# q in rows of 6 KB, row-tiled transposes and a new token order in an attention kernel with a token mixer

## Chip, cores, metric

One core of one Trainium2 chip. The metric is the device time of one execution in microseconds. Times are medians of several executions; every ratio to the kernel before uses executions on the same chip in the same rounds.

## The reference

```python
# q (8, 16, 384, 64), k and v (8, 4, 384, 64), scaled by 0.1; w_out (1024, 1024)
k = np.repeat(k, 4, axis=1); v = np.repeat(v, 4, axis=1)
scores = np.matmul(q, k.transpose(0, 1, 3, 2)) / np.sqrt(64)
attn = softmax(scores)                                    # over the last axis
x = np.matmul(attn, v).transpose(0, 2, 1, 3).reshape(8, 384, 1024)
wq, wk = x @ w_q, x @ w_k                                 # (8, 384, 64)
W_tok = wq @ wk.T / np.sqrt(64)                           # per batch, (384, 384)
out = np.maximum(W_tok @ x, 0.0) @ w_out                  # float32
```

The kernel never forms W_tok. It computes wk^T x first (`mix_c`), then multiplies by wq (`mix_m`), then by w_out (`po`).

One warning for all that follows. The scores are so small that the softmax is nearly flat, and the rows of a batch of the result differ from their mean by only 0.9% (norm, worked out from the reference). Rows stored in wrong places give an error of 1.3%, which the comparison of the runs let pass. So "correct" in these runs says that values are right, and says nothing of the order of the tokens. Where an experiment puts rows in wrong places on purpose this is said; where it claims the right order, that follows from the indices, not from a run.

## The kernel before

A Python function writes one fixed order of instructions per engine. It keeps a small model of the clocks of the engines (`clk`, `ready`) and at each step issues the TensorE work that the model calls ready. If nothing is, it issues filler matmuls (`keep_busy`) that hold the array's clock up. The parts that matter, with cuts marked:

```python
def load(b):                                   # q: three tokens per partition and head, 768 B
    def ld(dst, src, a, z, c0=0, c1=C):
        nc.sync.dma_start(out=dst[:, a:z, c0:c1],
                          in_=src[b, a:z].rearrange("h (p c) d -> p h c d", p=P)[:, :, c0:c1])
    # ... b == 0: k, q in slices of c, v, by halves of the heads; else k, q, q, v

def tr_q(b, blocks):                           # full 128x128 transposes, one PSUM bank, one copy
    # ...
    nc.tensor.transpose(out=ps[:, n * G + j, :], in_=qb[:, c, kp, j]..., identity=ident)
    nc.vector.tensor_copy(out=QT[:, t0:t0 + 2 * G, :], in_=ps)

def scores(b, s):                              # two heads side by side in row tiles, then exp
    nc.tensor.matmul(out=ps[:, u, :], lhsT=KT[lo:hi, kp * C + kc, :],
                     rhs=QT[lo:hi, t0:t0 + G, :].rearrange("k i p -> k (i p)"), ...)
    nc.scalar.activation(out=pt..., in_=ps, func=AF.Exp, scale=attn_scale)

def po():                                      # output projection, copy to SBUF, store
    dst = out[b].rearrange("(p c) n -> c p n", c=C)[c]
    # ...
    nc.sync.dma_start(out=dst, in_=osb)        # 128 rows of 4 KB
```

A chain per batch (`chain_open`) goes x transposes, `wqk`, `wk_tr`, `mix_c`, four `mix_m`, then 48 `po` matmuls. K and Q of batches 2 to 7 and most of x are transposed by DMA; the first two batches and the last third of each x by TensorE.

The softmax here doesn't subtract the row's maximum and nothing guards it: scores larger than these inputs give would overflow.

Of the kernel before, what the change touches and what calls it, by code (L numbers as in the profile page):

```python
# [15 lines left out]
def kernel(  # L16
# [17 lines left out]

    nc = tc.nc
# [9 lines left out]
    NH = 512  # L45
    KP = Hkv // 2
# [3 lines left out]
    NWIDE = 0  # L50
    NB = 4
    NPT = 9
    EAGER = 1
    DMA_TR = 5500
# [24 lines left out]
    clk = {"pe": 0.0, "dve": 0.0, "act": 0.0}  # L79
    mode = ["full"]  # L80
    wide_ps = [psG.tile([P, 2, NH], F32, name=f"wide{i}") for i in range(NWIDE)]
    bank_ps = [psG.tile([P, NH], F32, name=f"bank{i}") for i in range(NB)]
    wide_free = [0.0] * NWIDE
# [16 lines left out]

    def when(*keys):
        return max(ready.get(key, INF) for key in keys)
# [4 lines left out]

    def wide():
        return min((f, i) for i, f in enumerate(wide_free))
# [12 lines left out]
    def load(b):  # L122
        kraw = raw_p.tile([P, Hkv, C, D], F32, name="kraw")
        vraw = raw_p.tile([P, Hkv, C, D], F32, name="vraw")
        qraw = raw_p.tile([P, Hq, C, D], F32, name="qraw")
        raws[b] = (kraw, vraw, qraw)

        def ld(dst, src, a, z, c0=0, c1=C):
            nc.sync.dma_start(out=dst[:, a:z, c0:c1],  # L129
                              in_=src[b, a:z].rearrange("h (p c) d -> p h c d", p=P)[:, :, c0:c1])  # L130

        half = Hq // KP
        if b == 0:
            ld(kraw, k, 0, 2)
            ld(qraw, q, 0, half, 0, 1)
            ld(qraw, q, 0, half, 1, C)
            ld(vraw, v, 0, 2)
            ld(kraw, k, 2, 4)
            ld(qraw, q, half, Hq)
            ld(vraw, v, 2, 4)  # L140
        else:
            ld(kraw, k, 0, 4)
            ld(qraw, q, 0, half)
            ld(qraw, q, half, Hq)
            ld(vraw, v, 0, 4)

    def cast_open(b):
        nats[b] = (nat_p.tile([P, KP, C, 2, D], BF16, name="kb"),
                   nat_p.tile([P, C, KP, G, 2, D], BF16, name="qb"))

    def cast_k(b, kp, eng):
        for u in range(2):
            eng.tensor_copy(out=nats[b][0][:, kp, :, u, :], in_=raws[b][0][:, 2 * kp + u])  # L153

    def cast_q(b, kp, eng):
        for u in range(2):
            h0 = (2 * kp + u) * G
            eng.tensor_copy(out=nats[b][1][:, :, kp, :, u, :].rearrange("p c i d -> p i c d"),  # L158
                            in_=raws[b][2][:, h0:h0 + G])

    def cast_qc(b, kp, c, u, copy):
        h0 = (2 * kp + u) * G
        copy(out=nats[b][1][:, c, kp, :, u, :], in_=raws[b][2][:, h0:h0 + G, c, :])

    def cast_v(b, kp, eng):
        eng.tensor_copy(out=vexts[b % 3][:, 2 * kp:2 * kp + 2, :, :D],
                        in_=raws[b][1][:, 2 * kp:2 * kp + 2])

    def cast(b):
        cast_open(b)  # L170
        for kp in range(KP):
            cast_k(b, kp, nc.gpsimd)
        for kp in range(KP):
            cast_q(b, kp, nc.gpsimd)
        for kp in range(KP):
            cast_v(b, kp, nc.gpsimd)
# [4 lines left out]
    def start_tr(b):  # L181
        KT = tr_p.tile([P, KP * C, P], BF16, name="KT")
        QT = tr_p.tile([P, C * KP * G, P], BF16, name="QT")
        trs[b] = (KT, QT)

    def tr_dma(b, part):
        kb, qb = nats[b]
        KT, QT = trs[b]
        if part == 0:
            nc.sync.dma_start_transpose(out=KT, in_=kb.rearrange("p a c u d -> p (a c u d)"))  # L190
            for kp in range(KP):
                ready["K", b, kp] = clk["pe"] + DMA_TR
        else:
            c, n = part - 1, KP * G
            nc.sync.dma_start_transpose(out=QT[:, c * n:(c + 1) * n, :],
                                        in_=qb[:, c].rearrange("p a i u d -> p (a i u d)"))
            for kp in range(KP):
                ready["Q", b, kp, c] = clk["pe"] + DMA_TR

    def tr_k(b, kp0, kp1):  # L200
        kb, _ = nats[b]
        KT, _ = trs[b]
        _, i = bank()
        ps = bank_ps[i].bitcast(BF16).rearrange("p (n t) -> p n t", n=8)
        n = 0
        for kp in range(kp0, kp1):
            for c in range(C):
                nc.tensor.transpose(out=ps[:, n, :], in_=kb[:, kp, c].rearrange("p u d -> p (u d)"),
                                    identity=ident)
                n += 1  # L210
        nc.vector.tensor_copy(out=KT[:, kp0 * C:kp1 * C, :], in_=ps[:, :n, :])
        done = bank_free[i] = on("dve", 360 if n == C else 560, pe(56 * n))
# [3 lines left out]
    def tr_q(b, blocks):  # L216

        _, qb = nats[b]
        _, QT = trs[b]
        _, i = bank()  # L220
        ps = bank_ps[i].bitcast(BF16).rearrange("p (n t) -> p n t", n=8)
        for n, (c, kp) in enumerate(blocks):
            for j in range(G):
                nc.tensor.transpose(out=ps[:, n * G + j, :],
                                    in_=qb[:, c, kp, j].rearrange("p u d -> p (u d)"), identity=ident)
        end = pe(56 * G * len(blocks))
        if len(blocks) == 2 and blocks[1][0] == blocks[0][0]:
            t0 = (blocks[0][0] * KP + blocks[0][1]) * G
            nc.vector.tensor_copy(out=QT[:, t0:t0 + 2 * G, :], in_=ps)
            done = on("dve", 690, end)  # L230
        else:
            for n, (c, kp) in enumerate(blocks):
                t0 = (c * KP + kp) * G
                nc.vector.tensor_copy(out=QT[:, t0:t0 + G, :], in_=ps[:, n * G:(n + 1) * G, :])
                done = on("dve", 420, end)
        bank_free[i] = done
        for c, kp in blocks:
            ready["Q", b, kp, c] = done


    def groups(b):
        if b == 0:
            return [(kp, c) for kp in range(KP) for c in range(C)]
# [6 lines left out]
    def scores(b, s):  # L250
# [5 lines left out]
        for u in range(2):  # L256
            lo, hi = u * D, (u + 1) * D
            t0 = (c * KP + kp) * G
            nc.tensor.matmul(out=ps[:, u, :], lhsT=KT[lo:hi, kp * C + kc, :],  # L259
                             rhs=QT[lo:hi, t0:t0 + G, :].rearrange("k i p -> k (i p)"),  # L260
# [10 lines left out]
    def attend(b, g, u):  # L271
# [3 lines left out]
        if g == 0 and u == 0:  # L275
            xnats[b] = x_p.tile([P, C, Hq, D], BF16, name="xnat", bufs=3)
# [3 lines left out]
        for i in range(G):  # L280
            for kc in range(C):
                nc.tensor.matmul(out=ps[:, i * DE:i * DE + D + 1], lhsT=tiles[kc][:, u, i, :],  # L282
                                 rhs=vext[:, 2 * kp + u, kc, :D + 1],
# [4 lines left out]
        h0 = (2 * kp + u) * G  # L288
        nc.vector.tensor_tensor(out=xnats[b][:, c, h0:h0 + G, :], in0=avv[:, :, :D],  # L289
                                in1=rcp.to_broadcast([P, G, D]), op=ALU.mult)  # L290
# [9 lines left out]
    def x_by_dma(b, c):  # L300
        return b > 0 and c < C - 1
# [8 lines left out]
    def x_tr_dma(b, c):  # L310
        x_open(b)
        xn = xnats[b].rearrange("p c h d -> p c (h d)")
        nc.sync.dma_start_transpose(out=xTs[b][:, :, c, :], in_=xn[:, c, :])
        ready["T", b, c] = when(("X", b, c, 0), ("X", b, c, 1)) + DMA_TR

    def x_tr(b, c):
        x_open(b)
        xn = xnats[b].rearrange("p c h d -> p c (h d)")
        _, i = bank()
        ps = bank_ps[i].bitcast(BF16).rearrange("p (n t) -> p n t", n=DC)  # L320
        for dc in range(DC):
            nc.tensor.transpose(out=ps[:, dc, :], in_=xn[:, c, dc * P:(dc + 1) * P], identity=ident)  # L322
# [326 lines left out]
```

## Time and profile before

| | before |
|---|---|
| median (lowest to highest) | 222.12 us (221.69 to 222.29) |
| span of the profiled execution | 224.3 us |
| TensorE busy | 95% |
| VectorE, ScalarE busy | 65%, 63% |
| mean granted clock | 0.985 |
| last matmul starts | 220.5 us |

The profiled execution took 226.12 us and is of the slow state, by 1.8%. Three groups of the page: output projection, scores, and the copy of a finished half tile. After the bar stand busy time and the mean length of one in ns, then the idle time of the engine before them.

```profile
L408 PE MATMUL bank<-wout_sb,msb 128*128 128x512 bf16 x357 | 91.7, 382 | 1.3 <-issue 0.5
...
L259 PE MATMUL sc<-QT,KT 64*128 64x512 bf16 x288 | 47.5, 387 | 3.1 <-DMA QT<-qb 2.9
...
L421 DVE COPY osb<-bank 128x512 f32<-128x512 f32 (+1 forms) x49 | 33.1, 677 | 21.7 <-PE bank L408 20.5
```

A matmul's record of 380 ns includes its way through the pipeline; back to back they start every 216 ns. The copy takes 0.69 us, so a store of two halves becomes ready every 16 x 0.216 = 3.46 us when nothing but projection runs.

### The profile page before, as it was taken

What the parts mean: (1) busy time and instruction counts of PE and PEld (TensorE: products, weight loads), DVE (VectorE), ACT (ScalarE), POOL (GpSimd) and SP (SyncE); (2) the same over time, 40 slices, a digit from 0 to 9 for tenths busy, and PEclk for the clock granted to TensorE, in tenths of its full rate; (3) what the DMA queues carried; (4) which work ended last, traced back from release to release, by engine and by line L of the source; (5) the groups of instructions that cost most, each with busy time, mean ns of one, the idle gap of its engine ahead of it and who ended that gap; (6) DMA issues with size and microseconds to landing.
All of it is one profiled execution on the core that took longest, in us unless ns stands there. A gap on an engine that the chain in (4) does not pass through costs nothing.

```text
span 224.3 us, 5470 instructions
## 1 busy us (share of the span) xinstructions
PE 214.2 (95%) x2217; PEld 113.6 (51%) x2244; DVE 145.2 (65%) x365; ACT 140.6 (63%) x146; POOL 52.1 (23%) x97
## 2 busy tenths in 40 slices
PE   8999999589999999999999999999999999999993
PEld 5666665245545545454555546554555553434441
DVE  2355786834697758865887648874679569576332
ACT  3599998747788778887887887887888600000000
POOL 1385678406300540045016100620000000000000
PEclk9999999959999999999999999999999999999999
DMA  6996999999399979999999998989224422242424
GB/s 174 324 327 170 410 386 325 136 237 323 65 183 215 335 166 187 222 338 216 223 229 342 154 213 260 281 205 154 99 91 53 143 93 93 93 190 93 180 101 187
DMA packets 71688, 46.09 MB, mean 205 GB/s; under 512 B 42736, under 2 KB 67568, under 8 KB 71664
## 3 DMA queue, kind: packets, MB, share of 16 engines
q1 hardware_dynamic: 71520, 45.62, 77.6%
q8 instruction: 17, 0.28, 0.5%
q10 hardware_dynamic: 144, 0.13, 0.2%
q14 instruction: 7, 0.06, 0.1%
HBM read 23.59 MB, written 12.58 MB: 161 GB/s over the span
## 4 chain that ended last, share of the span: by engine, by line
PE 74%; DMA 14%; DVE 3%; SPq 3%; POOL 3%; issue 1%; DVEq 0%
PE bank L408 37%; PE bank L282 13%; PE sc L259 12%; DMA qraw<-in_q_dram 12%; PE bank L331 4%; SPq L129 3%; PE bank L384 3%; PE bank L362 2%; DMA QT<-qb 2%; PE bank L322 1%; POOL qb L158 1%; DVE osb L421 1%; PE bank L349 1%; DVE msb L389 1%; POOL wqk_sb L596 1%
## 5 line engine op out<-in xcount | busy, mean ns | idle before, releaser
L263 ACT ACTIVATE pt<-sc 128x1024 bf16<-128x1024 f32 x144 | 138.9, 1023 | 34.6 <-PE sc L259 34.4
L408 PE MATMUL bank<-wout_sb,msb 128*128 128x512 bf16 x357 | 91.7, 382 | 1.3 <-issue 0.5
L408 PEld LDWEIGHTS <-msb 128*128 128x128 bf16 x384 | 33.8, 98 | 42.4 <-issue 13.7
L259 PE MATMUL sc<-QT,KT 64*128 64x512 bf16 x288 | 47.5, 387 | 3.1 <-DMA QT<-qb 2.9
L282 PEld LDWEIGHTS <-pt 128*128 128x128 bf16 x1152 | 41.9, 98 | 15.8 <-issue 9.9
L282 PE MATMUL bank<-vext,pt 128*128 128x65 bf16 x1152 | 46.9, 195 | 0.4 <-DVE osb L421 0.2
L421 DVE COPY osb<-bank 128x512 f32<-128x512 f32 (+1 forms) x49 | 33.1, 677 | 21.7 <-PE bank L408 20.5
L289 DVE TENSOR_TENSOR xnat<-bank,rcp 128x256 bf16<-128x256 f32 x96 | 40.8, 425 | 3.3
L389 DVE TENSOR_SCALAR msb<-bank 128x384 bf16<-128x384 f32 x64 | 32.5, 551 | 9.5 <-PE bank L384 9.0
L287 DVE RECIPROCAL rcp<-bank 128x4 f32<-128x4 f32 x96 | 16.9, 176 | 17.6 <-PE bank L282 16.7
L158 POOL CAST qb<-qraw 128x768 bf16<-128x768 f32 x30 | 24.0, 827 | 17.4 <-DMA qraw<-in_q_dram 15.1
L153 POOL CAST kb<-kraw 128x192 bf16<-128x192 f32 x30 | 9.2, 347 | 67.3 <-DMA kraw<-in_k_dram 67.3
L259 PEld LDWEIGHTS <-KT 64*128 64x128 bf16 x288 | 12.4, 94 | 24.1 <-issue 17.2
L117 PE MATMUL bank<-idle 128*128 128x256 bf16 x80 | 14.8, 324 | 1.0 <-DVE idle L562 1.0
L331 PE MATMUL bank<-xT,wqk_sb 128*128 128x384 bf16 x64 | 11.7, 327 | 0.0
L117 PEld LDWEIGHTS <-idle 128*128 128x128 bf16 x80 | 7.9, 114 | 6.6 <-issue 4.0
L384 PE MATMUL bank<-wT,Csb 64*128 64x384 bf16 x32 | 10.6, 332 | 0.4 <-DVE rcp L287 0.3
L384 PE MATMUL bank<-wq,Csb 64*128 64x384 bf16 x32 | 10.6, 332 | 0.0
L599 POOL CAST wout_sb<-wld 128x1024 bf16<-128x1024 f32 x8 | 8.1, 1040 | 4.1 <-DMA wld<-in_moe_w_out_dram 4.1
L366 DVE CAST Csb<-bank 128x512 bf16<-128x512 f32 x8 | 5.5, 688 | 5.2 <-PE bank L362 5.2
L337 DVE CAST wT<-bank 128x384 bf16<-128x384 f32 x8 | 4.5, 558 | 6.7 <-PE bank L331 6.7
L323 DVE COPY xT<-bank 128x1024 bf16<-128x1024 bf16 x10 | 6.9, 688 | 2.5 <-PE bank L322 2.5
(33 smaller groups left out, 70.1 us busy)
## 6 DMA issues: line engine op xcount, KB each, us to landing
out_dram<-osb SPq DMA_DIRECT2D x23, 512.0 KB, 3.1
qraw<-in_q_dram SPq DMA_DIRECT2D x15, 768.0 KB, 7.4
wld<-in_moe_w_out_dram SPq DMA_DIRECT2D x4, 1024.0 KB, 9.5
kraw<-in_k_dram SPq DMA_DIRECT2D x7, 384.0 KB, 4.3
vraw<-in_v_dram SPq DMA_DIRECT2D x7, 384.0 KB, 8.9
qraw<-in_q_dram SPq DMA_DIRECT2D x1, 512.0 KB, 5.3
kraw<-in_k_dram SPq DMA_DIRECT2D x2, 192.0 KB, 3.7
vraw<-in_v_dram SPq DMA_DIRECT2D x2, 192.0 KB, 6.3
```

What stands on the lines that cost most here:

```text
L117: nc.tensor.matmul(out=bank_ps[i][:, :256], lhsT=idle[:, :P], rhs=idle, start=True, stop=True)
L158: eng.tensor_copy(out=nats[b][1][:, :, kp, :, u, :].rearrange("p c i d -> p i c d"), in_=raws[b][2][:, h0:h0 + G])
L259: nc.tensor.matmul(out=ps[:, u, :], lhsT=KT[lo:hi, kp * C + kc, :], rhs=QT[lo:hi, t0:t0 + G, :].rearrange("k i p -> k (i p)"), start=True, ...
L263: nc.scalar.activation(out=pt.rearrange("k u i p -> k u (i p)"), in_=ps, func=AF.Exp, scale=attn_scale)
L282: nc.tensor.matmul(out=ps[:, i * DE:i * DE + D + 1], lhsT=tiles[kc][:, u, i, :], rhs=vext[:, 2 * kp + u, kc, :D + 1], start=(kc == 0), sto ...
L287: nc.vector.reciprocal(out=rcp, in_=avv[:, :, D])
L289: nc.vector.tensor_tensor(out=xnats[b][:, c, h0:h0 + G, :], in0=avv[:, :, :D], in1=rcp.to_broadcast([P, G, D]), op=ALU.mult)
L331: nc.tensor.matmul(out=ps, lhsT=wqk_sb[:, dc, :], rhs=xT[:, dc].rearrange("d c p -> d (c p)"), start=(dc == 0), stop=(dc == DC - 1))
L384: nc.tensor.matmul(out=bank_ps[i][:, :S], lhsT=Csb[lo:hi, j * P:(j + 1) * P], rhs=w[lo:hi, :], start=True, stop=True)
L389: nc.vector.tensor_scalar_max(out=msb[:, dc, :], in0=bank_ps[i][:, :S], scalar1=0.0)
L408: nc.tensor.matmul(out=ps, lhsT=msbs[b][:, dc, c * P:(c + 1) * P], rhs=wout_sb[:, dc, half * NH:(half + 1) * NH], start=(nd == 0), stop=(n ...
L421: nc.vector.tensor_copy(out=osb[:, n0:n1], in_=ps[:, n0 - half * NH:n1 - half * NH])
```

## The change

The intent: q comes in packets of 6 KB instead of 768 B; TensorE's transposes are done as pairs of 64-row tiles, next to the scores, which use the same tiling; the x transposes of a batch start while its attention still runs; x has its columns in natural order. The price is a new order of tokens: a partition of q now holds one of 16 groups `s` of 24 tokens, so a tile of 128 queries has its column at `m * 16 + s`, and a tile's row goes to token `s * 24 + c * 8 + m` of the result. The core of the diff:

```diff
-        qraw = raw_p.tile([P, Hq, C, D], F32, name="qraw")
+        qraw = raw_p.tile([P, 2, C * M, D], F32, name="qraw")
+            src = q[b].rearrange("(u a) (s t) d -> (a s) u t d", u=2, t=C * M)
+            nc.sync.dma_start(out=qraw[:, :, c0 * M:c1 * M], in_=src[:, :, c0 * M:c1 * M])
 ... cut: casts by c, loads of batch 2 in the prologue, the model's DMA and GpSimd clocks
+    def half_trs(srcs):
+        two = [bank(half)[1] for half in range(2)]
+        for j, src in enumerate(srcs):
+            for half in range(2):
+                lo, hi = half * H, (half + 1) * H
+                nc.tensor.transpose(out=outs[half][:, j, :], in_=src[lo:hi], identity=ident[lo:hi, lo:hi])
+        return outs, two, pe(n * 29.5, "row")
+    def half_copies(outs, two, end, dsts, ns):
+                nc.vector.tensor_copy(out=dst[:, :, half * H:(half + 1) * H], in_=outs[half][:, n0:n1, :])
 ... cut: tr_k, tr_q, x_tr by these two; groups of batch 0 in the order of the others
-                             rhs=QT[lo:hi, t0:t0 + G, :].rearrange("k i p -> k (i p)"),
+                             rhs=QT[lo:hi, c * M:(c + 1) * M, kp * H:(kp + 1) * H].rearrange(
+                                 "k m (i s) -> k i m s", i=G),
 ... cut: xnat in natural column order; chain_open at the first attention of a batch
-        return b > 0 and c < C - 1
+        return b > XPE and c < C - 1          # XPE = 1: batch 1's x by TensorE too
 ... cut: wk_tr in a row tile
-        dst = out[b].rearrange("(p c) n -> c p n", c=C)[c]
+        dst = out[b].rearrange("(s c m) n -> c m s n", c=C, m=M)[c]
-                (...).dma_start(out=dst[:, n0:n1], in_=osb[:, n0:n1])
+                (...).dma_start(out=dst[:, :, n0:n1], in_=osb[:, n0:n1])
 ... cut: constants of the planner
```

## The prediction

> **What bounds the kernel now.** I read the busy line of the page first, then the 40 slices, then a table of windows, then the chain of waits around the one hole that the slices show, and last the groups, which give the duration of each operation that the change touches. The busy line and three rows of slices:
>
> ```profile
> PE 214.2 (95%) x2217; PEld 113.6 (51%) x2244; DVE 145.2 (65%) x365; ACT 140.6 (63%) x146; POOL 52.1 (23%) x97
> ...
> PE   8999999589999999999999999999999999999993
> ...
> ACT  3599998747788778887887887887888600000000
> ...
> PEclk9999999959999999999999999999999999999999
> ```
>
> TensorE looks full, but one slice (the eighth, 39 to 45 us) is half empty, the ninth runs at half clock, and ScalarE is at 9 only from about 11 to 34 us. So there are two regimes. In the first, the exponentials set the pace: the first starts at 7.55 us, there are 18 per batch at 1.023 us, so two batches last until about 7.5 + 36 x 1.023 = 44.3 us. In the second, from 50 us on, TensorE does. To see whether it is really full there, I add the work after 50 us at its best rates, read off the timeline and the chain: 383 output projections x 0.216 = 82.7; 36 blocks of 24 attention matmuls x 0.79 = 28.4; 104 score pairs x 0.216 = 22.5; some 52 score bursts x 0.2 of mode change (0.1 each way, from the spacings below) = 10.4; seven chains (wq/wk 1.30, mix_c 0.97, mix_m 0.74, two sets of transposes 0.45 and 0.165) x 3.6 = 25.4. Sum 169.4 us, against 50 to 221, less about 1.7 of tail: 169. So after 50 us nothing but less TensorE work can help, and before it every useful microsecond done earlier shortens the end by as much.
>
> What TensorE did before that is not useful: the windows of the filler matmuls (columns: window, length, busy, count, clock, DMA share, GB/s) and the wait for batch 2:
>
> ```profile
> 7.00:26.00 19.00, 6.78 (x45) 1.00 0.95 295
> 26.00:44.00 18.00, 1.00 (x6) 1.00 1.15 302
> 44.00:50.00 6.00, 1.24 (x5) 0.51 1.00 221
> ```
>
> ```profile
> 24.88 14.96 DMA qraw<-in_q_dram
> 39.90 1.60 POOL qb L158 x2
> 41.53 3.79 DMA QT<-qb
> 45.45 0.61 PE sc L259 x2
> ```
>
> The chain of waits says it plainly: batch 2's q lands at 39.8, is cast by 41.5, transposed by DMA until 45.3, and only then do its scores start. TensorE stood for 2.87 us, then ran at a clock of 0.51 until about 50. ScalarE lost 2.6 us too, but it isn't the bound afterwards. Of the window 44 to 50, I count about 2.4 us of useful work at full rate (three score pairs with their mode changes 1.3, one attention block 0.8, one mix_m pair 0.2), so **3.6 us are lost** there.
>
> **What the Trainium skill says.** "TensorE: Matmul & The Clock Gate", Part 1, says that an idle window of about 3.4 us drops the array to half rate and that it takes as long to come back; the trace agrees: clock 0.51 from 44 to 50, and a score burst of four taking 0.61 instead of the usual 0.54 spacing. "TensorEngine Tiling (Array Packing)", Key Properties, says a change of tiling mode drains TensorE while different tiles run in parallel; the trace agrees: four score matmuls in row tiles take 0.43 us when tiled work follows and 0.53 when full-array work does. "DMA: Bandwidth & Descriptors", Why small descriptors are slow, charges each packet and descriptor an overhead; the trace shows 322 to 327 GB/s while the q rows of 768 B load (5 to 15 us), and 415 when the 4 KB weight rows do (25 to 30 us). The same page, How many engines (k), says that a transfer runs on the largest number up to 16 that divides the outermost dimensions of both sides; the trace of before, whose stores have 128 outermost, can't test it, but the new store has 8 outermost on the DRAM side. That is a risk, below.
>
> **The change, part by part.**
> *Loads.* q in one packet of 6 KB per partition and head pair (2 KB in batch 0) instead of 768 B. Up to q of batch 2 the queue carries three batches of 2.36 MB and 4.7 MB of weights, 11.8 MB, done at 39.8 us. At about 325 GB/s for the 2.4 MB of k and v and 405 for the other 9.4: 7.3 + 23.2 + 2 for the start = 32.5 us. Batch 2's load and casts are also issued in the prologue, instead of after batch 1's first score. Then 1.1 us of cast and 3.8 us of DMA transpose give its first scores at about 37 to 38 us, well before ScalarE asks for them at 44. So the hole and the slow clock go: **minus 3.6 us**.
> *Weights.* w_out is fully cast at 36.1 us before; with the queue faster, and GpSimd not held by late q, I put it at 28 to 30.
> *Transposes.* These lines give what TensorE pays now:
>
> ```profile
> L322 PE MATMUL bank<-ident,xnat 128*128 128x128 bf16 x80 | 6.1, 220 | 0.0
> ...
> L224 PE MATMUL bank<-ident,qb 128*128 128x128 bf16 x48 | 4.1, 228 | 0.0
> ...
> L349 PE MATMUL bank<-ident,wT 128*128 128x128 bf16 x24 | 2.6, 219 | 0.2 <-DVE wT L337 0.2
> ...
> L208 PE MATMUL bank<-ident,kb 128*128 128x128 bf16 x12 | 1.3, 241 | 0.0
> ```
>
> The mean of 220 ns is latency; eight in a row take 0.45 us, so 56 ns each, 164 x 0.056 = 9.2 us. After, a 128x128 block is two half transposes of 64 rows side by side, each streaming 64 columns instead of 128. The attention matmuls stream 65 columns at 0.79/24 = 33 ns, so I estimate 30 to 33 ns a block (the source assumes 29.5). Blocks after: 60 for q and k, x three sets each for batches 0 and 1 and one for each of six others, 12 x 8 = 96, and 24 small ones: 180 x 0.030 = 5.4. **Minus 3.8 us** in all; of it 6 x 0.21 for x of later batches, 0.2 for the last set of batch 1 and 7 x 0.075 for wk, that is 2.0, fall into the full regime. The rest falls where ScalarE paces, and only turns into filler.
> *x transposes inside attention, group order.* The chain of batch 0 may start during its attention. Its x transposes then fill holes before 26 us in which 45 filler matmuls run now; wq/wk start near 28.5 instead of 33.1; mix_m is done by 34 or 35. From then to 44 us TensorE is free for what scores and attention leave. In 26 to 44 us the needed work is 18 score pairs with mode changes 7.5, six attention blocks 4.7, the chain 3.7: 16 of 18 us. So some 2.2 us of output projection, ten matmuls, moves ahead of 44 us, where today none stands before 49.98; and the mix_m work that now straddles the hole, 0.35, moves with it: **minus 2.5 us**.
> *Costs.* Two half copies of 420 ns replace one of 690 on VectorE (512 columns cost 420 now, 1024 cost 690): 18 or so x 0.15 = 3 us more on an engine that is 65% busy; beside other work. Two more x sets on TensorE, 0.5, inside the slack. q's first slice is 512 KB before the first score instead of 256, some 0.4 us later, but with one pair of copies in its path; the first exponential stays near 7.3, and the gap of 1.06 us after the third should go, which ScalarE, not the end, feels.
> Sum: 3.6 + 2.0 + 2.5 = 8.1 us. A second way: useful TensorE work of before, 169.4 + 33.2 up to 50 us, is 202.6; less 3.8 it is 198.8; start 7.1, tail 1.7, and 4.8 of filler that stays before 33 us since nothing else is ready: 212.4. From 222.1 the first gives 214.0. I take **213.5 us**.
>
> **Rivals.**
> (a) *DMA becomes the bound.* Between 60 and 160 us the DMA share is 0.91 to 1.06 at only some 230 GB/s, because each batch has six DMA transposes: I estimate 2 us of all engines each, from the stretch 160 to 175 us. The q rows take off about 1 us a batch. But if the stores ran on 8 engines, those would carry 2.8 us instead of 1.4 per store (from 175 us on there are stores alone, 132 GB/s at a share of 0.35, so 377 GB/s, and 0.52 MB take 1.4), 4.2 more per batch of 21.4: transposes would come late and TensorE, whose order is fixed in the program, would stall at the scores of batches 3 to 6. Against it: nothing on TensorE waits for DMA after 50 us now, and the whole batch is loaded ahead. If true: 216 to 222 us.
> (b) *The hole only moves.* If GpSimd, not the load, holds batch 2 (eight w_out casts of 1.04 stand ahead of it), its scores would wait to 45 again; the gain would be 3 to 5, 217 to 219. For: one engine does all casts. Against: 52 us busy in all, and it waits for DMA most of the first 40.
> (c) *Row-tiled transposes cost as much as full ones* (16 instructions instead of 8, two banks instead of one): the 2 us vanish, 215.5; with waits for banks 217. The score matmuls' new pattern in runs of 16 columns could also stream slower; every 10% is 3 us. Nothing in the trace speaks for it.
>
> **Range and chances.** The hole (3.6) is the surest term; the early projections (2.5) depend on the planned order meeting real times; (a) is the heaviest risk. Everything better than expected, with half the remaining filler gone, gives 209. One rival true gives up to 218. So 209 to 218; faster by over 2% (under 217.7) 0.87, within 2% 0.09, slower 0.04.
>
> **What would show it right or wrong.** The slice at 40 to 50 us should be full at full clock, with no wait of the scores for QT there; q of batch 2 landed by 34 us; first output projection near 35; the x transposes' groups at about 0.25 us per set of eight blocks; filler about 60 matmuls instead of 80. Wrong if the scores of batches 3 to 6 wait for QT, if stores land in over 4 us instead of 2.9, or if score pairs take more than 0.22.

## More of the kernel before

The page's DMA part has, per kind of transfer, the size and the median time from issue to landing:

```profile
out_dram<-osb SPq DMA_DIRECT2D x23, 512.0 KB, 3.1
qraw<-in_q_dram SPq DMA_DIRECT2D x15, 768.0 KB, 7.4
```

A store lands 3.1 us after its issue, less than the 3.46 us in which the next one is made.

## The result

| | before | after |
|---|---|---|
| median, same chip and rounds | 222.2 us | 234.46 us (231.88 to 236.67) |
| ratio of fast executions | | 1.0488, interval 1.0357 to 1.0619 |
| span of the profiled execution | 224.3 us | 234.9 us |
| last VectorE copy starts, before the end | 3.5 us | 9.1 us |
| score matmuls waiting for QT | 2.9 us, one wait, at 42 to 45 us | 6.4 us, two waits, at 111 and 161 us |

A ratio is the mean time of one kernel's fast executions over that of the other's in the same rounds, so it isn't quite the ratio of the medians. The profiled execution after is slow, as the one before was; its two holes and its tail are what the comparison below rests on, and they were tested in fast executions of other kernels. Its three fast executions have granted clocks of 0.971, 0.973 and 0.985 against the slow one's 0.971.

The page after, the busy line and the three rows of slices (each now 5.9 us):

```profile
PE 215.6 (92%) x2414; PEld 111.2 (47%) x2414; DVE 146.9 (63%) x384; ACT 141.0 (60%) x146; POOL 53.1 (23%) x110
...
PE   5999999999999999998599999995999999999940
...
ACT  3599989686878778867277788674577800000000
...
PEclk9999999999999999999889999998899999999995
```

The old hole at the eighth slice is gone: TensorE is full from 6 us on. (The 9s of PEclk at the very start say only that no throttling is recorded there. The trace's record of the clock begins where full rate is granted, at 9.59 us here and at 6.61 in the kernel before; until then four score matmuls take 1.03 us instead of 0.60.) But there are two new dips, at slices 20 and 28, each with a lower clock behind it, and the end has one slice at 4 and one at 0. The table of windows shows the same; its columns are window, length, busy time of TensorE, its weight loads, VectorE, ScalarE and GpSimd with counts, clock, DMA share, GB/s:

```profile
60.00:80.00 20.00, 20.00 (x248) 10.77 (x248) 14.47 (x39) 16.48 (x18) 1.53 (x5) 1.00 1.07 230
100.00:120.00 20.00, 16.48 (x169) 8.14 (x168) 11.56 (x29) 11.63 (x13) 3.72 (x8) 0.91 1.06 158
...
160.00:175.00 15.00, 12.10 (x135) 6.05 (x134) 8.21 (x24) 8.75 (x10) 0.00 (x0) 0.89 0.66 109
```

A window without a hole is full (20 of 20; so is 140 to 160 us); the two with one lack 3.5 and 2.9 us, and their clocks of 0.91 and 0.89 mean 3.6 and 3.3 us at half rate. The list of waits and the chain name the cause:

```profile
PE sc L277 <- DMA QT<-qb: 6.4, 2, 3.5
```

```profile
104.57 9.73 DMA QT<-qb
114.99 1.39 PE bank L426 x4
```

The first hole's link is shown; the second, at 154 us, has a transpose of 9.06 us. A transpose of Q for the next batch takes 9 to 10 us from issue to landing, where the kernel before had a median of 3.7. This is what the prediction had asked to be looked for as a sign that it is wrong. And the end, each kernel from its last copy of 256 columns on (before, then after):

```profile
222.00:223.00 1.00, 0.00 (x0) 0.00 (x0) 0.00 (x0) 0.00 (x0) 0.00 (x0) 1.00 0.78 262
223.00:225.00 2.00, 0.00 (x0) 0.00 (x0) 0.00 (x0) 0.00 (x0) 0.00 (x0) 1.00 0.00 0
```

```profile
226.00:228.00 2.00, 0.00 (x0) 0.00 (x0) 0.51 (x2) 0.00 (x0) 0.00 (x0) 1.00 0.52 123
228.00:230.00 2.00, 0.00 (x0) 0.00 (x0) 0.00 (x0) 0.00 (x0) 0.00 (x0) 0.51 0.44 155
230.00:232.00 2.00, 0.00 (x0) 0.00 (x0) 0.00 (x0) 0.00 (x0) 0.00 (x0) 0.50 0.43 155
```

Before, the last bytes have left by 223 us, 2.2 us after that copy. After, DMA works for another 6 us at 123 to 155 GB/s and a share of 0.43 to 0.52, while every engine is idle but for VectorE's last two copies. A share that sticks near one half of 16 engines hints at 8 engines, all busy. Two counts bear it out. The last quarter store is the only transfer on ScalarE's queue, so its line counts exactly that transfer (packets, MB, share), first before, then after:

```profile
q10 hardware_dynamic: 144, 0.13, 0.2%
```

```profile
q10 hardware_dynamic: 136, 0.13, 0.2%
```

128 rows of 1 KB, and 16 more packets before, 8 more after: I read these as completion writes, one of 4 bytes from each engine that takes part. In the whole trace the packets of 4 bytes fall from 2289 to 1889. The number of transfers changed too, so this alone proves little, but in the first two experiments below, where only the store's pattern differs, the count differs by 208 = 26 stores x 8. The other count is of packets of 4 KB in flight at once, worked out from the starts and lengths in the trace. In the changed kernel exactly 8 are in flight for 75% of the time from 212 to 224 us, and 10 or more for under 1%; in the kernel before, from 203 to 217 us, 16 or 17 are for 78% of the time in which any is.

### The profile page after: what moved, and what is told of

Its sections match the earlier page's. It is cut to its first block, busy times and chain, and to the rows that moved or that the text cites. A ratio compares the mean times of both kernels' runs of the same rounds, so it can differ in the third digit from the quotient of the medians.

```text
span 234.9 us, 5869 instructions
## 1 busy us (share of the span) xinstructions
PE 215.6 (92%) x2414; PEld 111.2 (47%) x2414; DVE 146.9 (63%) x384; ACT 141.0 (60%) x146; POOL 53.1 (23%) x110
## 4 chain that ended last, share of the span: by engine, by line
PE 73%; DMA 11%; ACT 5%; issue 3%; POOL 2%; DVE 1%; SPq 1%; POOLq 0%; DVEq 0%
PE bank L426 33%; PE sc L277 14%; PE bank L302 13%; DMA QT<-qb 8%; ACT pt L282 5%; PE bank L348 4%; PE bank L128 4%; DMA qraw<-in_q_dram 3%; PE bank L402 3%; PE bank L380 2%; PE bank L234 2%; POOL qb L180 1%; DVE osb L439 0%; DVE msb L407 0%; PE bank L366 0%
## 5 line engine op out<-in xcount | busy, mean ns | idle before, releaser
L282 ACT ACTIVATE pt<-sc 128x1024 bf16<-128x1024 f32 x144 | 139.1, 1023 | 43.3 <-PE sc L277 43.0
L426 PE MATMUL bank<-wout_sb,msb 128*128 128x512 bf16 x384 | 97.0, 384 | 0.0
L277 PE MATMUL sc<-QT,KT 64*128 64x512 bf16 x288 | 48.4, 390 | 6.8 <-DMA QT<-qb 6.4
L426 PEld LDWEIGHTS <-msb 128*128 128x128 bf16 x384 | 32.7, 98 | 42.0 <-issue 12.1
L180 POOL CAST qb<-qraw 128x512 bf16<-128x512 f32 x45 | 25.9, 619 | 24.4 <-issue 14.4
L307 DVE RECIPROCAL rcp<-bank 128x4 f32<-128x4 f32 x96 | 16.9, 176 | 14.5 <-PE bank L302 14.1
L240 DVE COPY xT<-bank 128x512 bf16<-128x512 bf16 x24 | 9.1, 419 | 3.6 <-PE bank L234 3.6
L402 PE MATMUL bank<-wq,Csb 64*128 64x384 bf16 x32 | 10.8, 338 | 0.0
L402 PE MATMUL bank<-wT,Csb 64*128 64x384 bf16 x32 | 10.8, 338 | 0.0
```

The source lines that it names most:

```text
L180: copy(out=nats[b][1][:, c * M:(c + 1) * M, u, :], in_=raws[b][2][:, u, c * M:(c + 1) * M])
L282: nc.scalar.activation(out=pt.rearrange("k u i p -> k u (i p)"), in_=ps, func=AF.Exp, scale=attn_scale)
L307: nc.vector.reciprocal(out=rcp, in_=avv[:, :, D])
L402: nc.tensor.matmul(out=bank_ps[i][:, :S], lhsT=Csb[lo:hi, j * P:(j + 1) * P], rhs=w[lo:hi, :], start=True, stop=True)
L426: nc.tensor.matmul(out=ps, lhsT=msbs[b][:, dc, c * P:(c + 1) * P], rhs=wout_sb[:, dc, half * NH:(half + 1) * NH], start=(nd == 0), stop=(n ...
```

## The experiments

Twelve kernels ran. All ratios are to the kernel before in the same rounds. At a margin of 2% the verdict on record is "same" for experiments 1, 8, 9 and 11, "slower" for 2 and "unclear" for 4 to 7 and 12; 3 and 10 have none, for want of fast executions. Small sizes read off "unclear" runs are estimates.

### 1. The changed kernel with the old store pattern

```diff
-        dst = out[b].rearrange("(s c m) n -> c m s n", c=C, m=M)[c]
+        dst = out[b].rearrange("(p c) n -> c p n", c=C)[c]
```

> The changed kernel with the store pattern of the kernel before (DRAM side 128 rows outermost instead of 8 by 16); rows of the result land in the wrong places on purpose. Theory (stores run on 8 of 16 engines, their backlog delays the DMA transposes and the last stores): the holes at 110-114 and 160-167 us go, the tail after the last matmul shrinks from 9 to about 3.5 us, time 211 to 216 us. Rival (two banks per transpose, half copies and one-engine casts cost the time): still above 225 us, holes stay. If the hole was only half of it: 217 to 224.

Measured: 222.22 us (219.53 to 222.35), ratio 0.9918, interval 0.9847 to 0.999. Rows are in wrong places. Both holes are gone and the tail is 3.5 us again. From its page, the busy line and the score matmuls' line:

```profile
PE 213.2 (97%) x2414; PEld 110.5 (50%) x2414; DVE 146.4 (66%) x384; ACT 140.7 (64%) x146; POOL 53.1 (24%) x110
...
L277 PE MATMUL sc<-QT,KT 64*128 64x512 bf16 x288 | 47.6, 387 | 0.3 <-ACT pt L282 0.3
```

The score matmuls' idle time is 0.3 us instead of 6.8. So the store pattern costs (1.0488 - 0.9918) x 223 = 12.7 us (give or take 3, since the changed kernel's own interval is 2.6% wide), and with it removed the change is worth 1.8 us by ratio, not the 8.6 that were forecast. The middle way of the expectation is what came: two questions, not one.

### 2. The kernel before with the new store pattern

```diff
-        dst = out[b].rearrange("(p c) n -> c p n", c=C)[c]
+        dst = out[b].rearrange("(s c m) n -> c m s n", c=C, m=8)[c]
```

> The kernel before with nothing changed but the store pattern of the changed kernel (8 by 16 rows, wrong places on purpose). Theory: the stores alone cost as much as they do in the changed kernel: 229 to 237 us, tail about 9 us instead of 3.5, waits of score matmuls for QT after 60 us. Rival (the store pattern is harmless, or harmful only with the other parts): 222 to 225 us.

Measured: 247.59 us (246.33 to 248.04), ratio 1.1074. Rows in wrong places. That is 24 us, twice what it costs in the changed kernel, and more than expected. Its list of waits:

```profile
PE sc L259 <- DMA QT<-qb: 16.9, 5, 6.8
```

Five waits instead of one. Why the harm is twice that in the changed kernel was not tested: that kernel's q arrives in larger packets, and its transposes are also issued two score steps earlier, so more of a delay may be hidden. What is shown is that the stores alone make either kernel slower.

### 3. Another column order, so that the store has 16 outermost

```diff
-                                 "k m (i s) -> k i m s", i=G),
+                                 "k m (i s) -> k i s m", i=G),
-        dst = out[b].rearrange("(s c m) n -> c m s n", c=C, m=M)[c]
+        dst = out[b].rearrange("(s c m) n -> c s m n", c=C, m=M)[c]
```

> The changed kernel with columns of a query tile ordered (s, m) instead of (m, s): the score matmuls read their moving operand with a step of 256 bytes instead of in runs of 16, and the store's DRAM side has 16 outermost (blocks of 32 KB). Result correct. Theory: stores on 16 engines, as the other run: 211 to 216 us, if the score pair stays at 0.216 us. Rival: single-element steps stream slower; at half speed the 144 pairs cost 31 us more, 240 us or so, though the tail still shrinks to 3.5 us.

Measured: 320.35 us (311.72 to 322.62). Only one execution is fast (311.72 us), so there is no ratio; an effect of 88 us needs none. The rival was right, and more so than it said:

```profile
L277 PE MATMUL sc<-QT,KT 64*128 64x512 bf16 x288 | 138.5, 1023 | 0.0
```

The record grew from 386 to 1023 ns. In the timeline two pairs take 1.88 us, of which the last record is 1.02, so a pair starts 0.86 us after the one before, where it took 0.216. The spans agree: the fast execution's 309.9 us is 89 us longer than experiment 1's 220.6, 0.62 us for each of 144 pairs. Reading the moving operand in runs of 16 elements (32 bytes) is free: 386 ns in both kernels. Reading it in single elements 256 bytes apart costs a factor of four.

### 4. Right order, each store in 8 transfers of 16 partitions

```diff
-            nc.sync.dma_start(out=dst, in_=osb)
+            for m in range(M):
+                (nc.scalar if last and m % 2 else nc.sync).dma_start(out=dst[m], in_=osb[m * 16:(m + 1) * 16, :])
```

> The changed kernel, result correct, each store issued as 8 transfers of 16 partitions (one per m, 16 outermost on both sides, the same scattered rows of 4 KB). Theory (the number of engines is what hurt): time as in the run with 128 rows outermost, within 1.5% of it (219 to 224 us), no score waits for QT, tail under 5 us, although SyncE issues 8 times as many transfers (8 x 0.35 = 2.8 us a store). Rival (the scatter of rows in DRAM hurts): 230 us or more. Third way: SyncE's queue becomes the bound and delays the transposes: 224 to 230 us with a short tail.

Measured: 245.73 us, ratio 1.1024: my theory in its first form fell. The number of completion writes is 4753, which is what 16 engines for each of the 192 pieces make (2097 in experiment 1, less 26 x 16, plus 192 x 16). So all 16 engines take part, and it is still slow. The tail after the last copy is 14.5 us, from which two windows:

```profile
234.00:236.00 2.00, 0.00 (x0) 0.00 (x0) 0.00 (x0) 0.00 (x0) 0.00 (x0) 0.50 0.77 141
...
238.00:240.00 2.00, 0.00 (x0) 0.00 (x0) 0.00 (x0) 0.00 (x0) 0.00 (x0) 0.50 0.84 144
```

Now the share is 0.77 to 0.84, so nearly all engines are busy, and yet they move 141 to 144 GB/s. A packet of 4 KB takes 369 ns on average there, against 162 ns at the end of the kernel before. The Trainium skill, "SBUF — State Buffer", Door 1: The DMA port swizzle, says that DMA bandwidth depends on how many of 16 ports the partitions reach, and that 16 neighbouring partitions reach four; it gives 104 GB/s for such a transfer at 1 MB. Our 141 to 144 GB/s from consecutive pieces of 64 KB fit this kind of limit and not the exact figure, since two pieces overlap. SyncE is a second reason: between 80 and 120 us the pieces of a store took 3.8 to 8.3 us to issue, not 2.8. The run can't separate the two for the middle of the kernel. In the tail the packets' length points to the first, but no run shows it apart from the small size of the pieces.

The rival, the scatter of rows in DRAM, came true in its number, but the scatter alone isn't the cause: the stores of experiment 8 write the same 128 rows each, in another order over 16 engines, and cost nothing that can be told; and in the changed kernel, with the scatter of this run, half of the packets take no more than 159 ns.

This changes the theory: what counts is the number of engines and what each packet then takes. At the ends, where only stores run, the trace's packets of 4 KB take on average:

| kernel | engines | packets per engine and store | ns per packet | us per store |
|---|---|---|---|---|
| before, 203 to 217 us | 16 | 8 | 162 | 1.30 |
| changed, 208 to 222 us | 8 | 16 | 224 | 3.58 |
| pieces of 16 partitions, 231 to 242 us | 16 | 8 | 369 | 2.95 |
| repaired (experiment 8), 200 to 212 us | 16 | 8 | 243 | 1.94 |

The last column is the product. For the pieces it is too small: their engines are busy only some 0.8 of the time, and at 141 to 144 GB/s 512 KB take 3.7 us. For the changed kernel 3.58 us is more than the 3.46 us in which TensorE makes the next store. So in the last 18 us, where the kernel is nothing but projection, DMA never gets free: when the last quarter store is issued, 0.88 MB are still to be moved, against 0.26 MB in the kernel before. At the 123 to 155 GB/s of the windows above, that is the tail.

### 5. ScalarE writes the exponentials in the other order

```diff
-        nc.scalar.activation(out=pt.rearrange("k u i p -> k u (i p)"), in_=ps,
+        nc.scalar.activation(out=pt.rearrange("k u i (s m) -> k (u i) m s", m=M),
+                             in_=ps.rearrange("k u (i m s) -> k (u i) m s", i=G, m=M),
```

> The changed kernel, result correct, with the exponentials written in (s, m) order by ScalarE's output pattern (steps of 16 bytes), so that a store has 16 outermost in blocks of 32 KB. If a stepped write costs ScalarE nothing (1.02 us each stays): as with 128 rows outermost, 219 to 224 us. If it halves ScalarE's rate: 2 us each, 144 of them, 300 us.

Measured: 710.23 us.

```profile
L282 ACT ACTIVATE pt<-sc 128x1024 bf16<-128x1024 f32 x144 | 654.2, 5069 | 5.4 <-PE sc L277 5.4
```

An exponential took 5.07 us instead of 1.02: a bf16 write with a step of 16 bytes costs ScalarE a factor of five, worse than the factor of two that I had allowed for. The Trainium skill, same page, SBUF "cachelines", says lines are 16 bytes and that at least two hits on a line are needed for the full rate. This run and experiment 3, where no two accesses share a line, agree in direction; the page gives no factor.

### 6. The transposes back in the full array

On top of experiment 1, planned order kept:

```diff
-            for half in range(2):
-                lo, hi = half * H, (half + 1) * H
-                nc.tensor.transpose(out=outs[half][:, j, :], in_=src[lo:hi], identity=ident[lo:hi, lo:hi])
+            nc.tensor.transpose(out=ps[:, j, :], in_=src, identity=ident)
```

> The changed kernel with stores of 128 rows outermost (wrong places on purpose), its PE transposes done in the full array again, 8 per set instead of 16 half ones, same planned order, same two copies. The prediction's step (2.0 us in the full regime, 3.8 in all): 2 to 4 us slower than the same kernel with half transposes. Rival (row tiles save little, the set takes 0.33 us where 0.24 was assumed): 0 to 1.5 us slower.

Measured: 226.0 us (224.22 to 226.18), ratio 1.0121. Against experiment 1 that is (1.0121 - 0.9918) x 223 = 4.5 us slower; the intervals are wide, so the size is rough. A second reading doesn't need the ratios: all four executions here have a clock of 1.0, three of them with spans of 224.1 to 224.4 us, and the three of experiment 1 at that clock have 220.3 to 220.6, so 3.9 us at equal clock (on two chips, where the kernel before at full clock differs by some 0.5 us). The reading of 1.0 leaves out the start, as said above. The prediction put 3.8 us of TensorE on the transposes in all (3.2 without the small ones of wk, which this run leaves in row tiles) but took only 2.0 of them into its sum; some 4 came back here. Its group (mean record 220 ns) and, from experiment 1's timeline, a set of 16 half transposes followed by projection:

```profile
L234 PE MATMUL bank<-ident,xnat 128*128 128x128 bf16 x96 | 7.4, 220 | 0.1
```

```profile
49.58 0.40 PE L234 MATMUL bank<-ident,xnat 64*128 64x64 bf16 x16
...
49.91 1.04 PE L426 MATMUL bank<-wout_sb,msb 128*128 128x512 bf16 x4
```

The set takes 49.91 - 49.58 = 0.33 us, with the change of mode back to the full array in it, where 0.24 without it was assumed; the full sets took 0.45 plus the change of mode after the scores.

### 7. The first q slice in two halves

On top of experiment 1: the first slice of q is loaded, cast and transposed by halves of 64 partitions.

```diff
-            ld_q(0, 1)
+            for half in range(2):
+                lo, hi = half * P // 2, (half + 1) * P // 2
+                nc.sync.dma_start(out=qraw[lo:hi, :, 0:M], in_=src[lo:hi, :, 0:M])
 ... cut: casts and transposes of one half each
```

> The changed kernel with stores of 128 rows outermost (wrong places on purpose), and the first q slice loaded, cast and transposed in two halves of 64 partitions, so that the first scores wait for 256 KB instead of 512. Theory (the late first exponential, 8.2 to 8.8 us against 7.55 before, costs its delay at the end): first exponential near 7.3, time 1 to 2 us less than the same kernel without it. Rival (the delay is absorbed by filler later): no difference within 0.5 us.

Measured: 220.67 us, ratio 0.9903 (0.9846 to 0.996), against 0.9918: no difference that the rounds can tell. That is the rival's number, but the run doesn't test its question. The first exponential came at 8.41 us and not near 7.3, while traces with the slice undivided have it anywhere from 7.88 (experiment 12) to 8.84 (experiment 1). So whether a late start costs time is not shown.

### 8. A repair in the right order

The mixer needs the token order of wk and x to agree with each other, but wq may have any order: its columns become the rows of the result. So only wq is reordered, by the copy out of PSUM that is made anyway.

```diff
-        nc.vector.tensor_copy(out=wT, in_=ps)
-        nc.vector.tensor_copy(out=wq2[Dh:2 * Dh, :], in_=ps[:Dh, :])
+        nc.vector.tensor_copy(out=wT[Dh:2 * Dh, :], in_=ps[Dh:2 * Dh, :])
+        nc.vector.tensor_copy(out=wT[:Dh, :].rearrange("h (c s m) -> h c s m", c=C, m=M),
+                              in_=ps[:Dh, :].rearrange("h (c m s) -> h c s m", c=C, m=M))
+        nc.vector.tensor_copy(out=wq2[Dh:2 * Dh, :], in_=wT[:Dh, :])
-        dst = out[b].rearrange("(s c m) n -> c m s n", c=C, m=M)[c]
+        dst = out[b].rearrange("(s c m) n -> c s m n", c=C, m=M)[c]
```

> The changed kernel with a correct repair: VectorE writes the wq half of wT in (s, m) order (it reads PSUM in steps of 16 elements, once per batch, 64 partitions), wk and x keep (m, s); so the out tokens come in (s, m) order and a store covers 128 partitions with 16 outermost in DRAM, blocks of 32 KB. Theory (a store must have 128 partitions and 16 engines): like the run with 128 rows outermost, ratio to before 0.985 to 1.0, 219 to 223 us, and 16 completion writes per store again. Rival (stepped PSUM reads are as slow as stepped SBUF accesses were): VectorE copy of 2 us or more on the chain, 223 to 227 us.

Measured over five rounds: 220.60 us (218.83 to 221.83) against 222.87, ratio 0.9901, interval 0.9855 to 0.9946. The 4-byte packets are 2097 again, as in experiment 1. The copies of wk (plain) and wq (stepped), in the view of the tile wT (durations: lowest, median, highest in ns):

```profile
L354 DVE CAST wT<-bank x8: 560/561/562, 32.5 to 186.6; 64x384 bf16<-64x384 f32 x8
L356 DVE CAST wT<-bank x8: 549/550/550, 33.1 to 187.2; 64x384 bf16<-64x384 f32 x8
```

Reading PSUM in steps of 64 bytes costs VectorE nothing. The store's packets are slower than before (243 ns, table above), but 1.94 us is well under 3.46. This is the fastest kernel that claims the right order, by the ratios 5.6% faster than the changed one. Against the one before it is 1.0% faster: the interval leaves out 1.

### 9. The repair and the halves together

> The same repair, and the first q slice in two halves of 64 partitions. Expected 0 to 1.5 us below the repair alone (the run of the halves alone gained 0.3 us by ratio, 1.5 by medians); 218.5 to 221.5 us. If it isn't below, the start is absorbed by filler.

The edits of 7 and 8 together. Measured: 221.41 us, ratio 0.9941 (0.9898 to 0.9985), so not better than the repair alone. Its first exponential, at 8.29 us, is no earlier either, so it settles no more than 7.

### 10. Stores from GpSimd's queue

```diff
-            nc.sync.dma_start(out=dst, in_=osb)
+            nc.gpsimd.dma_start(out=dst, in_=osb)
```

> The changed kernel with its 8-by-16 stores (all but the last ones) issued from GpSimd's queue instead of SyncE's. If that queue also uses the same 8 engines: 232 to 240 us. If it spreads stores over all 16 engines in turn, 219 to 226 us. It also takes stores out of SyncE's queue, where transposes wait behind them; GpSimd spends time on descriptors, so casts may come later.

Measured: 234.25 us; three of four executions slow, the fast one 227.38. The trace shows another kind of queue with 2944 packets of 4 KB, of 159 ns median as in the changed kernel, and QT landing 8.7 us after its issue, so it isn't a repair. Which engines it used can't be told, but its stores aren't spread over all 16 at once: from 205 to 225 us exactly 8 packets are in flight for 53% of the time, and 14 or more for about 1%.

### 11. Batch 1's x by DMA again

On top of experiment 1: `XPE = 0` instead of 1.

> The changed kernel with stores of 128 rows outermost (wrong places on purpose) and batch 1's first two x sets transposed by DMA again, as before the change. My accounting says these two sets take 0.67 us of TensorE in the very place (44 to 50 us) where the hole was: so 0.3 to 1 us faster than with them. Rival: the DMA transposes come late and delay the chain of batch 1: 0.5 us slower or more.

Measured: 221.19 us, ratio 0.9931 (0.9892 to 0.9969), next to experiment 1's 0.9918. The gain of 0.3 to 1 us that I expected isn't seen: no effect of the two sets can be told.

### 12. Only the last batch's stores in the old pattern

```diff
+        if b == B - 1:
+            dst = out[b].rearrange("(p c) n -> c p n", c=C)[c]
```

> The changed kernel with only the last batch's three stores in the pattern of 128 rows outermost (those rows in wrong places on purpose); the other 21 stores stay 8 by 16. My split of the 14 us: about 5.6 us are the tail (9.1 us after the last matmul against 3.5), the rest the two holes. So the tail goes and the holes stay: 5 to 6 us less than the changed kernel, ratio to before 1.02 to 1.03, 227 to 230 us. Rival (the holes alone make the loss and the tail merely follows): less than 2 us gained.

Measured: 227.98 us (227.27 to 228.63), ratio 1.0232. Three stores of 24 are worth (1.0488 - 1.0232) x 223 = 5.7 us (give or take 3), which fits the tail (9.1 - 3.5 = 5.6 us; here it is 3.5 again). Two dips stay in its slices, with 4.4 us of waiting for QT. The other 12.7 - 5.7 = 7.0 us are then the holes, by subtraction, and fit 6.4 us of waiting plus part of the half-rate time.

## Why the prediction was wrong, point by point

**The store.** The step that failed is rival (a). It named the cause, read from the skill's rule about k and from the diff, and then gave it too little weight, for a reason that was no reason: "nothing on TensorE waits for DMA after 50 us now". That tells of a margin, not of its size, and the DMA share near 1 in the same window told that it was small. What runs showed in its place: stores on 8 engines cost 12.7 us, some 7 as waits for QT and 5.7 as the tail. The waits came at the first scores of batches 5 and 7 (180 and 252 score matmuls of 36 a batch stand before them), not at each of 3 to 6. Its size was also wrong three times. It took 2.8 us per store, twice 1.4, because half the engines do the work; measured were 16 packets x 224 ns = 3.58. It never compared a store with the 3.46 us in which TensorE makes one, so the tail, 5.7 us, is missing. And its "216 to 222" became 234.5.

**The hole.** Right in that it went: TensorE is busy for 94% of the time or more, at full clock, from 39 to 50 us in the changed kernel. q of batch 2 had landed by 35.5 us in experiment 1, where I gave 34, and was cast by 39, ahead of the need. Its worth was mis-sized, because the 3.6 us were read from a slow execution (226.12 us) and taken off the median of fast ones (222.12). The kernel before ran 32 times more beside the experiments, and each execution has a span and a mean clock. They fall into three groups, the same on all four chips:

| granted clock | executions | mean span | state |
|---|---|---|---|
| 0.999 to 1.0 | 16 | 220.6 us | fast |
| 0.992 | 10 | 222.2 us | fast |
| 0.985 | 6 | 224.0 us | slow |

The profiled execution (0.985, 224.3 us) is of the last group; its windows show the half rate from about 44.15 to 50.98 us, 6.8 us, and 6.8 x 0.5 / 224.3 = 0.015 is the whole deficit. A clock of 0.992 is one half of that, 1.0 none, so I read the groups as two, one or no stretch of some 3.4 us at half rate. Only an execution of the last group was traced: where the one stretch of the middle group lies isn't shown, and in experiments 7 and 8, traced at 0.992, it lies at the start (7.1 to 10.8 us). The Trainium skill, "TensorE: Matmul & The Clock Gate", Part 1, calls its window free-running and the ramp "run-variable"; these groups fit that. On this reading the half rate costs 224.0 - 220.6 = 3.4 us in the slow group, and on average over the fast ones (16 with none, 10 with 1.6 us) only 0.6. Of the 3.6 us that the prediction took off, 3.4 - 0.6 = 2.8 were never in the time that it took them from. No trace of the kernel before at full clock was taken, so whether the scores' wait of 2.9 us is as long there is open. Two of the prediction's readings there are off. The 0.61 us of a score burst is for two matmuls, not four (at full rate two take 0.39). And the clock fell 1.6 us after the last work before the hole had ended (42.58 us), so only the length of the slow stretch, 6.83 us or twice 3.41, matches the windows that it names.

**Projections ahead of 44 us.** Wrong: 2.5 us were forecast. In experiment 1 four projection matmuls stand before 44 us and nine before 50, against ten and none. Filler was to fall to 60 matmuls and stayed at 78; in the changed kernel they lie here (columns as in the prediction's table of the kernel before):

```profile
7.00:26.00 19.00, 5.92 (x34) 1.00 1.04 358
26.00:44.00 18.00, 2.98 (x18) 1.00 0.92 277
44.00:50.00 6.00, 0.83 (x6) 1.00 0.81 311
```

26 to 44 us has 18 fillers where it had 6. The step that failed is "wq/wk start near 28.5 ... mix_m is done by 34 or 35": in experiment 1 wq/wk start at 32.09, and the last mix_m at 47.18. The timeline of experiment 1, one line for each link of batch 0's chain (start, length; mix_c, not shown, starts at 36.36 and takes 0.84):

```profile
29.94 0.40 PE L234 MATMUL bank<-ident,xnat 64*128 64x64 bf16 x16
...
32.09 1.47 PE L348 MATMUL bank<-xT,wqk_sb 128*128 128x384 bf16 x8
...
38.54 0.32 PE L402 MATMUL bank<-wT,Csb 64*128 64x384 bf16 x1
...
41.38 0.60 PE L426 MATMUL bank<-wout_sb,msb 128*128 128x512 bf16 x2
```

From the last x transpose to the first projection 11.4 us pass, though the five links together are 4 us of TensorE. Between them lie copies of 0.25 to 0.76 us on VectorE, and scores and attention of batch 1, which go first. I had added up TensorE time where a chain of dependent steps sets the pace. So in the time that the hole gave back little other work was ready: from 44 to 50 us experiment 1 did five projections, two scores and two mix_m matmuls more than the kernel before, 1.6 us, two x sets that DMA had done before, 0.7, and filler of 0.9 (the kernel before is here the slow execution, the only one traced). Experiment 11, without the two sets, has 12 projections before 50 us instead of nine, but its time shows no gain.

**Transposes.** Right in kind, too small in the sum: 2.0 of 3.8 us were taken into the time, on the ground that the rest only turns into filler; experiment 6 shows 3.9 to 4.5. Why the rest counted too isn't shown.

**The first exponential.** It was to stay near 7.3 us; it came at 8.2 in the changed kernel and 8.84 in experiment 1. The larger slice isn't the whole reason: in the changed kernel the transposes of q start at 5.83 us, in the kernel before at 5.90, but full rate is granted 3 us later, so filler and scores take longer. Whether it matters isn't shown, as experiments 7 and 9 didn't bring it forward.

**The sum without the store.** 8.1 us were forecast; experiments 1 and 8 give 1.8 and 2.2 us by ratio. Take 2.8 off for the state and up to 2.5 for the projections (four of ten came), and 2.8 are left, of which 2.0 are the transposes. That is near what was measured, but it isn't the whole account: at an equal reading of the clock (1.0) experiment 1's spans of 220.3 to 220.6 us are hardly shorter than the 220.5 to 221.3 of the kernel before on the same chip, though experiment 6 says that its transposes save about 4. So something gives back most of it: later start, more filler before 44 us, two x sets more, or the order of the plan. Experiment 11 took away the third without a gain that can be told. The start deserves a look: in experiment 1's trace, which reads 1.0, full rate is first granted at 12.79 us, against 6.61 in the kernel before, and the reading counts none of this; the executions at 0.992 of experiments 7 and 8 (the traced ones at full rate from 10.5 and 10.8 us on) have spans of 218.5 to 219.3 us, shorter than experiment 1's at 1.0. No run changed the start or the plan alone; this part stays open.

## What to carry to other kernels

When a change touches a transfer's access pattern, look at the outermost sizes of both sides first, and compare the time of one transfer with the interval in which the program makes them, not with the share of busy time. Count a chain of dependent small steps by its latencies, with the copies between them, before you promise that its end will fill a hole, and take a loss off a time only if both are of the same state. A reordering that has to be paid somewhere was cheapest here where an engine copies out of PSUM anyway, on the smallest tensor that carries the order.

## What the Trainium skill lacked or had wrong

- "TensorE: Matmul & The Clock Gate", Part 1, tells of the run-to-run variation at a kernel's start and says not to fit to it. Here the same kernel had spans of 220.6, 222.2 and 224.0 us in 16, 10 and 6 executions, in step with mean clocks of 1.0, 0.992 and 0.985, and the one that was traced had its half rate (6.8 us) after a hole in the middle. That is more than the change without its stores is worth.
- "DMA: Bandwidth & Descriptors", How many engines (k): the rule held. A store with 8 outermost in DRAM and 128 partitions made 8 completion writes, with 128 or 16 outermost 16. The page doesn't say that a store on 8 engines costs more than twice: 3.58 us against 1.30 for 512 KB, since a packet takes 224 ns instead of 162 on average.
- The same page, Rules for kernel authors, advises all 16 engines, with the 128 partitions outermost as the ideal, and doesn't say what fewer partitions cost; k = 16 on 16 partitions was no better here (ratio 1.1024, 369 ns per packet). A likely reason is on "SBUF — State Buffer", Door 1; the rule could point there. That section's 104 GB/s at 1 MB for 16 partitions was 141 to 144 GB/s here with several pieces under way.
- "SBUF — State Buffer", SBUF "cachelines": no factors. Here: moving operand of bf16 in runs of 32 bytes, no loss (386 ns); single elements with a step of 256 bytes, about four times (0.86 us against 0.216 a pair); ScalarE's bf16 writes with a step of 16 bytes, five times (5.07 against 1.02 us).
- The same place warns of PSUM steps for matmuls and is silent on VectorE: a read of fp32 in steps of 64 bytes took 550 ns against 560 to 561 for a plain one.
- No page that I read gives the time of a row-tiled transpose: a set of 16 half transposes (eight 128x128 blocks) took 0.33 us with the change of mode, against 0.45 in the full array without it.
